# A linear-attention and gated-MLP kernel: five engines in a written order, weights decoded a whole block at a time, five PSUM banks in turn

## The chip, the cores and the metric

One core of one Trainium2 chip. The metric is the device time of one execution in microseconds (us), the median of several runs. Engine names as in the profile: PE is TensorE (matmuls; PEld its weight loads), DVE VectorE, ACT ScalarE, POOL GpSimd, SP SyncE, which here only issues transfers.

## What is computed

A recurrence per batch and head over 768 tokens, whose output feeds a gated MLP:

```python
for t in range(S):                                   # B, H, S, D = 4, 8, 768, 48
    cur = einsum('bhd,bhe->bhde', u * k[t], v[t])
    y[t] = einsum('bhd,bhde->bhe', r[t], state + cur)
    state = w * state + einsum('bhd,bhe->bhde', k[t], v[t])
x = y as (3072, 384)
out = (sigmoid(x @ w_gate) * (x @ w_val)) @ w_out    # d_ff = 1536
```

## The kernel before

**Attention.** The 768 tokens are 12 chunks of 64, and the heads 2 halves, so there are 24 *groups* `n` in order, two for a chunk. A group has these steps. `load` brings its channel-major (`chan`) and token-major (`toks`) inputs, three buffers of each. `prepare` scales queries (POOL, tile `dec`), bonus keys (four ACT instructions) and keys (DVE), and `prepare_tokens` the token-major keys (POOL). `scores` is 64 small matmuls; `keep` copies the two masked halves of the scores to SBUF (DVE); `apply` is 32 matmuls with the state (`by_state`), 32 for the state's increment (`outer`) and 32 with the scores (`by_scores`), with a drain of PE behind the first 32; `advance` updates the state (four DVE instructions); `to_x` writes the result as a high half (ACT) and a low half (DVE) into `xt`, and `fill` moves 16 rows of it with small transfers.

**MLP.** Two chunks make a *tile* of 512 columns, so there are 6 tiles. `d_ff` is 12 blocks `f`. An *item* is one block for one tile: `up` (18 matmuls of 512 columns, 9 into a gate bank and 9 into a value bank of PSUM), `gate` (sigmoid on ACT, product on DVE, high half on ACT, low half on POOL), and one item later `down` (9 matmuls into the accumulators `acc0` to `acc2`). Every product is made of three f32r matmuls of high and low halves. In tile 0 the first `HALF` = 4 blocks are done for 256 columns at a time, first for chunk 0, then for chunk 1: 8 half items, 8 whole ones.

**Weights.** They come as 64-bit words, 12 blocks of 1152 words per partition, each block in two halves of 576. For each half, `scale_words` (ACT) scales the upper 32 bits, `join_words` (three DVE instructions: a left shift with one source, then two instructions with two sources that put in sign and low bits), and `split_weights` makes the high half `whi` (ACT) and the rest `wlo` (POOL). `load_weights(f)` is issued at item f-2 and `decode(f)` follows in item f-1.

**PSUM.** `two_banks()` is a pool of two buffers, each of two banks, taken by `up`, `scores`, `apply` and small work: four banks, beside three for the accumulators.

**Order.** PE and SP run in the order in which the program is written; DVE, ACT and POOL in an order that a scheduler chose with its own estimates. SP issues every transfer: inputs, weights, `fill`, and the output. Which group goes into which item is in `SLOTS0` (tile 0) and `SLOTS` (items 0, 3, 6, 9 of the later tiles). A group's place in an item is: `up`, `scores`, `gate`, `keep`, `down` of the item before, `apply`, `to_x`, `advance`, then loads and `prepare` of the next.

Of the kernel before, what the change touches and what calls it, by code (L numbers as in the profile page):

```python
# [10 lines left out]
F32 = mybir.dt.float32  # L11
# [9 lines left out]
P = 128  # L21
# [24 lines left out]
def rwkv_then_moe(ctx: ExitStack, tc: tile.TileContext, wd, ch, tk, wt, rk0, vn0, wd0, out):  # L46
# [6 lines left out]
    op = ctx.enter_context(tc.tile_pool(name="op", bufs=2))  # L53
    ps = ctx.enter_context(tc.tile_pool(name="ps", bufs=2, space=PSUM))
# [7 lines left out]

    def two_banks():
        return ps.tile([P, 2, 512], F32, name="ring")
# [3 lines left out]
    order.enter_context(tc.manual_schedule(engines={mybir.EngineType.PE, mybir.EngineType.SP}))  # L68
# [9 lines left out]
    def load(n):  # L78
        c, g = GROUPS[n]
        chan[n] = ach.tile([P, 2, 512], F32, name="chan")  # L80
        nc.sync.dma_start(out=chan[n], in_=ch[c, g])
# [25 lines left out]
    table = const.tile([P, 1], F32, name="table")
    nc.scalar.activation(table, ident[:, 0:1], AF.Sigmoid)
# [4 lines left out]
    nc.vector.memset(pw[:, :, 0], 1.0)  # L113
    nc.vector.tensor_scalar(pw[:, :, 1], w, 0.5, 2.0, ALU.max, ALU.min)
# [18 lines left out]


    tabn = const.tile([P, N2, D], F32, name="tabn")
    flag = const.tile([1, 1], I32, name="flag")

    def token_table():
        power(32, 32, 32)
        power(64, 32, 64)  # L140
        rev = hp.tile([P, 512], F32, name="sg").rearrange("q (p a j) -> q p a j", p=NP, a=2)
        pws = pw.rearrange("q (p s) j -> q p s j", p=NP)
        nc.vector.tensor_copy(rev[0:64], pws[0:64, :, :, 95:31:-1])
        for gm in range(2):
            nc.vector.tensor_copy(rev[64:128, :, gm], pws[64:128, :, 1 - gm, 95:31:-1])
# [25 lines left out]

    W3, WH = 3 * DM, 3 * DM // 2
    raw, w32, whi, wlo = {}, {}, {}, {}

    def load_weights(f):
        for j in range(2):
            t = raw[f, j] = wp.tile([P, WH], I64, name="wr", tag=f"w{2 * f + j}")
            nc.sync.dma_start(out=t, in_=wt[f, :, j * WH : (j + 1) * WH])

    def scale_words(f, j):  # L180
        g = w32[f, j] = wtmp.tile([P, WH], F32, name="wf")
        words = raw[f, j].bitcast(F32).rearrange("q (n two) -> q n two", two=2)
        nc.scalar.activation(g, words[:, :, 1], AF.Copy, scale=2.0**-112)

    def join_words(f, j):
        words = raw.pop((f, j)).bitcast(I32).rearrange("q (n two) -> q n two", two=2)
        low, high = words[:, :, 0], words[:, :, 1]
        g = w32[f, j].bitcast(I32)
        nc.vector.tensor_scalar(g, g, 3, None, ALU.logical_shift_left)
# [3 lines left out]
    def split_weights(f):  # L193
        whi[f] = wp.tile([P, W3], F32R, name="whi", tag=f"w{2 * f}")
        wlo[f] = wp.tile([P, W3], F32R, name="wlo", tag=f"w{2 * f + 1}")
        for j in range(2):
            c, g = slice(j * WH, (j + 1) * WH), w32.pop((f, j))
            nc.scalar.copy(out=whi[f][:, c], in_=g)
            nc.gpsimd.tensor_tensor(wlo[f][:, c], g, whi[f][:, c], ALU.subtract)  # L199

    def decode(f):
        for j in range(2):
            scale_words(f, j)
        for j in range(2):
            join_words(f, j)
        split_weights(f)
# [13 lines left out]
    def prepare(n):  # L220
        c, g = GROUPS[n]
        t = dec[n] = adk.tile([P, 2, 512], F32, name="dec")
        r, k = chan[n][:, 0], chan[n][:, 1]
        tab = tabk[:, 4 * g : 4 * g + 4]
        nc.gpsimd.tensor_tensor(v4(t[:, 0]), v4(r), bc2(tab[:, :, ::-1]), ALU.mult)  # L225
# [5 lines left out]
        nc.vector.tensor_tensor(v4(k), v4(k), bc2(tab), ALU.mult)  # L231
# [29 lines left out]
    def apply(n):  # L261
        c, g = GROUPS[n]
        y = yb[n] = two_banks()
        k, v, t = toks[n][:, 0], toks[n][:, 1], score[n % 2]
        begun = set()

        def mm(half, bank, m, cs, lhsT, rhs, stop):
            first = (half, bank) not in begun
            begun.add((half, bank))
            nc.tensor.matmul(  # L270
                y[64 * half : 64 * half + m, bank, cs], lhsT, rhs,
                start=first, stop=stop, skip_group_check=True,
            )

        def by_state(half, p, p2):
            for be in range(2):
                s, row, m = half, slice(64 * be, 64 * be + D), D if half else 64
                at = (4 * (2 * g + p) + 2 * s + p2) * D
                i = (4 * p + 2 * s + p2) * C
                mm(half, be, m, slice((2 * p + p2) * C, (2 * p + p2 + 1) * C),  # L280
                       state[row, at : at + m], dec[n][row, 0, i : i + C], False)


        def outer(half, p, p2):
            for gm in range(2):
                row, at = slice(64 * gm, 64 * gm + 64), (4 * p + 2 * half + p2) * D
                m, o = D if half else 64, 256 + (2 * p + p2) * D
                mm(half, gm ^ half, m, slice(o, o + D), k[row, at : at + m],
                       v[row, at : at + D], True)

        def by_scores(half, p, p2):
            for gm in range(2):
                be, row = gm ^ half, slice(64 * gm, 64 * gm + 64)
                m, at = D if half else 64, (4 * p + 2 * be + p2) * D
                i = (4 * be + 2 * p + p2) * C
                mm(half, be, m, slice((2 * p + p2) * C, (2 * p + p2 + 1) * C),
                       v[row, at : at + m], t[row, i : i + C], True)

        units = []
        if c:  # L300
            units += [(by_state, p, p2) for p, p2 in PP]
        if c < NC - 1:
            units += [(outer, p, p2) for p, p2 in PP]
        units += [(by_scores, p, p2) for p, p2 in PP]
        turned = False
        for f, p, p2 in units:
            if f is not by_state and c and not turned:

                nc.tensor.drain()
                turned = True  # L310
            for half in range(2):
                f(half, p, p2)

    def advance(n):
        c, g = GROUPS[n]
        if c == NC - 1:
            return
        y, n2 = yb[n], 2 * D
# [380 lines left out]
```

## Time and profile before

| | |
|---|---|
| median of 3 runs | 626.62 us (626.25 to 627.57) |
| the profiled execution | 626.12 us, its span 624.1 us |
| PE busy | 543.8 us (87%), 5770 matmuls |
| PEld busy | 441.5 us (71%) |
| DVE busy | 219.9 us (35%), 365 instructions |
| ACT busy | 173.0 us (28%), 343 instructions |
| POOL busy | 201.5 us (32%), 161 instructions |
| DMA | 44.54 MB, 71 GB/s over the span |

The span runs from the first to the last instruction; the 2.0 us between it and the execution's time lie outside. A row of a timeline has start, length, engine, line, operation, tiles (written<-read) and how many were merged into it; in brackets stands the idle time before and what ended it. A row of instruction groups has the busy time in us and the mean of one in ns. PE's matmuls are pipelined, so one lasts longer than the distance to the next.

### The profile page before, as it was taken

The numbers are of one execution on the slowest core, as the hardware profiler recorded it, in microseconds if no ns is written. First come the engines' busy times: TensorE is split into PE (matmuls) and PEld (weight loads), VectorE is DVE, ScalarE is ACT, GpSimd is POOL, SyncE is SP. The second block draws the span as 40 slices with busy tenths as digits, with TensorE's granted clock in tenths as the row PEclk, the third lists the DMA queues.
The fourth block names the chain that finished last, engine by engine and source line by source line (L and its number), as shares of the span: only waits on it lengthen the run. The fifth ranks groups of instructions, "written<-read, shape, count | busy, mean of one in ns | idle before, by whom it ended". The sixth has DMA issues, their size and how long they took to land. (4 is left out here: it accounts for less than half of the span.)

```text
span 624.1 us, 13029 instructions
## 1 busy us (share of the span) xinstructions
PE 543.8 (87%) x5770; PEld 441.5 (71%) x5770; DVE 219.9 (35%) x365; ACT 173.0 (28%) x343; POOL 201.5 (32%) x161
## 2 busy tenths in 40 slices
PE   2342566879999999999999999999999999999994
PEld 2232456757787787778778778777877777888883
DVE  7832999952223313232312332222232122111011
ACT  3312445531223212132212223213233111222121
POOL 6512667751332313143213224213313111212120
PEclk9997779989999999999999999999999999999998
DMA  8025765202024002114002212010240001000001
GB/s 332 6 68 184 288 254 199 92 0 71 2 78 173 1 1 69 18 62 171 2 2 68 79 58 116 1 42 28 79 170 3 1 9 17 25 28 0 2 0 54
DMA packets 14700, 44.54 MB, mean 71 GB/s; under 512 B 2256, under 2 KB 2640, under 8 KB 14640
## 3 DMA queue, kind: packets, MB, share of 16 engines
q1 hardware_dynamic: 14640, 43.66, 20.2%
q8 instruction: 47, 0.77, 0.5%
q14 instruction: 13, 0.11, 0.0%
HBM read 36.58 MB, written 4.72 MB: 66 GB/s over the span
## 5 line engine op out<-in xcount | busy, mean ns | idle before, releaser
L386 PE MATMUL ring<-xt,whi 128*128 128x512 f32 (+1 forms) x912 | 279.2, 389 | 0.0
L386 PE MATMUL ring<-xt,wlo 128*128 128x512 f32 (+1 forms) x456 | 180.5, 396 | 34.9 <-POOL wlo L199 15.7
L386 PEld LDWEIGHTS ring<-xt,whi 128*128 128x128 f32 x912 | 173.3, 195 | 35.9 <-DVE xt L354 0.2
L399 POOL TENSOR_TENSOR h<-sg,h 128x512 fp32r<-128x512 f32 (+1 forms) x76 | 97.0, 1277 | 298.8 <-ACT h L398 298.7
L397 DVE TENSOR_TENSOR sg<-ring,sg 128x512 f32<-128x512 f32 (+1 forms) x76 | 50.3, 662 | 267.9 <-ACT sg L396 267.9
L386 PEld LDWEIGHTS ring<-xt,wlo 128*128 128x128 f32 x456 | 88.8, 195 | 54.2 <-POOL wlo L199 15.9
L409 PE MATMUL acc<-h,whi 128*128 128x512 f32 (+1 forms) x456 | 115.6, 384 | 1.2 <-POOLq L525 0.6
L396 ACT ACTIVATE sg<-ring 128x512 f32<-128x512 f32 (+1 forms) x76 | 43.7, 575 | 229.2 <-PE ring L386 229.2
L409 PEld LDWEIGHTS acc<-h,whi 128*128 128x128 f32 x456 | 84.3, 192 | 19.3 <-POOL h L399 1.3
L409 PE MATMUL acc<-h,wlo 128*128 128x512 f32 (+1 forms) x228 | 67.3, 395 | 2.5 <-ACT h L398 2.5
L398 ACT CAST h<-sg 128x512 fp32r<-128x512 f32 (+1 forms) x76 | 45.4, 598 | 54.0 <-DVE sg L397 54.0
L225 POOL TENSOR_TENSOR dec<-chan,tabk 128x512 f32<-128x512 f32 x24 | 32.7, 1364 | 80.9 <-DMA chan<-in_ch 76.6
L409 PEld LDWEIGHTS acc<-h,wlo 128*128 128x128 f32 x228 | 40.9, 190 | 12.3 <-ACT h L398 3.4
L228 ACT ACTIVATE dec<-chan,wu 128x128 f32<-128x128 f32 x96 | 31.1, 392 | 65.3 <-DMA chan<-in_ch 57.4
L199 POOL TENSOR_TENSOR wlo<-wf,whi 128x576 fp32r<-128x576 f32 x24 | 40.3, 1695 | 25.8 <-issue 11.9
L231 DVE TENSOR_TENSOR chan<-chan,tabk 128x512 f32<-128x512 f32 x24 | 19.8, 824 | 73.6 <-ACT dec L228 73.6
L255 DVE COPY_PREDICATED score<-masks,ring 128x512 f32<-128x512 int32 x48 | 35.8, 745 | 1.0 <-PE ring L247 0.3
L270 PE MATMUL ring<-score,toks 64*64 64x64 f32 (+1 forms) x768 | 18.6, 233 | 15.2 <-DVE score L255 14.4
L237 POOL TENSOR_TENSOR toks<-toks,tabn 128x384 f32<-128x384 f32 x22 | 29.2, 1332 | 6.9 <-DMA toks<-in_tk 3.8
L354 DVE TENSOR_TENSOR xt<-ring,xt 112x512 fp32r<-112x512 f32 (+1 forms) x26 | 17.9, 688 | 32.5 <-ACT xt L353 32.2
L270 PEld LDWEIGHTS ring<-score,toks 64*64 64x64 f32 (+1 forms) x768 | 15.4, 136 | 16.2 <-DVE score L255 15.4
L353 ACT CAST xt<-ring 112x512 fp32r<-112x512 f32 (+1 forms) x26 | 15.2, 586 | 39.5 <-PE ring L270 34.1
(47 smaller groups left out, 274.6 us busy)
## 6 DMA issues: line engine op xcount, KB each, us to landing
wr<-in_wt SPq DMA_DIRECT2D x24, 576.0 KB, 7.8
chan<-in_ch SPq DMA_DIRECT2D x24, 512.0 KB, 3.8
toks<-in_tk SPq DMA_DIRECT2D x24, 400.0 KB, 4.2
out_y<-o SPq DMA_DIRECT2D x18, 256.0 KB, 2.4
xt<-xt SPq DMA_DIRECT2D x30, 64.0 KB, 2.3
xt<-xt SPq DMA_DIRECT2D x12, 32.0 KB, 2.5
wu<-in_wd SPq DMA_DIRECT2D x1, 8.0 KB, 1.7
```

Source lines behind the costliest of these rows:

```text
L199: nc.gpsimd.tensor_tensor(wlo[f][:, c], g, whi[f][:, c], ALU.subtract)
L225: nc.gpsimd.tensor_tensor(v4(t[:, 0]), v4(r), bc2(tab[:, :, ::-1]), ALU.mult)
L228: nc.scalar.activation(t[:, 1, cs], k[:, cs], AF.Copy, scale=wu[:, 1, 4 * g + m : 4 * g + m + 1])
L237: nc.gpsimd.tensor_tensor(v4(k), v4(k), bc2(tabn[:, 4 * g : 4 * g + 4]), ALU.mult)
L255: nc.vector.copy_predicated(t.rearrange("q (b m i) -> q b m i", b=2, m=4), masks[:, m].bitcast(I32).unsqueeze(1).unsqueeze(1).broadcast_to ...
L270: nc.tensor.matmul(y[64 * half : 64 * half + m, bank, cs], lhsT, rhs, start=first, stop=stop, skip_group_check=True,)
L386: nc.tensor.matmul(o[:, g, self.cols], w[a][:, g * DM + kt * P : g * DM + (kt + 1) * P], self.x[:, kt, b, self.cols], start=(k == 0), stop ...
L396: nc.scalar.activation(sg[:, c], o[:, 0, c], AF.Sigmoid)
L397: nc.vector.tensor_tensor(sg[:, c], o[:, 1, c], sg[:, c], ALU.mult)
L398: nc.scalar.copy(out=h[:, 0, c], in_=sg[:, c])
L399: nc.gpsimd.tensor_tensor(h[:, 1, c], sg[:, c], h[:, 0, c], ALU.subtract)
L409: nc.tensor.matmul(self.acc[d][:, self.cols], w[a][:, 2 * DM + d * P : 2 * DM + (d + 1) * P], h[:, b, self.cols], start=(f == 0 and k == 0 ...
```

## The change

All five engines now run in a written order. For tile 0 and groups 0 to 8 it is a list of steps, `START`; for the later tiles it is a loop. The drawn-out parts of the old functions are steps of their own, with one letter each. Loads come first in the order. `fill` is issued by ACT in place of SP. The decode of blocks 1 to 11 is done on 1152 words at a time (`WHOLE`), that of block 0 in halves; the rounding and the rest stay in halves. The left shift has a second source now, a zero that is broadcast. `HALF` is 1: tile 0 has two half items and 11 whole ones. The state is decayed on ACT (four instructions) and added to on DVE (one). From group 8 on (`FIRST`) the matmuls with the state come ahead of the scores, without a drain. The ring is one PSUM tile of five banks, of which each request takes the next two, the fifth together with the first.

```diff
-HALF = 4
-SLOTS0 = {0: 2, 2: 3, 4: 4, 7: 5, 10: 6, 13: 7}
+HALF, FIRST = 1, 8
 SLOTS = (0, 3, 6, 9)
-LOADW = (-2, -1, 0, 1, 2, 3, 4, 5, 6, 7, 8, 9)
-DECW = (-1, 0, 1, 2, 3, 4, 5, 6, 7, 8, 9, 10)
+START = """
+tk tc L.0 L.1 X.0 A.0 ti.1 R.0 X.1 ti.0 A.1 R.1 k.0 W.0 tp Z.0 K.0 tt tn L.2 T.0 k.1 I.0 Z.1 h.0
+X.2 T.1 c0.0 l.0 O.0 c0.1 K.1 L.3 F.0 A.2 R.2 s.0 X.3 T.2 k.2 I.1 j0.0 Z.2 h.1 W.1 A.3 R.3 O.1
+l.1 T.3 w0.0 s.1 F.1 K.2 o0.0 W.2 k.3 I.2 j0.1 c.1 Z.3 h.2 O.2 d.2 K.3 W.3 w0.1 l.2 c.2 o0.1 s.2
+F.2 j.1 I.3 L.4 U.0 h.3 d.3 X.4 O.3 g.0 l.3 W.4 w.1 m.0 R.4 F.3 s.3 H.0 j.2 A.4 U.1 q.0 o.1 W.5
+g.1 D.0 m.1 w.2 T.4 k.4 U.2 H.1 c.3 q.1 W.6 o.2 j.3 Z.4 g.2 D.1 c.4 L.5 U.3 m.2 w.3 X.5 K.4 H.2
...
+w.9 l.6 s.6 F.6 H.7 o.9 K.7 U.8 j.10 q.7 c.11 I.7 g.8 m.8 w.10 D.7 j.11 H.8 o.10 h.7 O.7 d.7 U.9
+l.7 q.8 w.11 s.7 F.7 o.11 D.8 g.9 m.9 H.9 L.8 X.8 U.10 q.9 D.9 g.10 m.10 H.10 U.11 q.10 D.10
+g.11 m.11 H.11 U.12 q.11 A.8 R.8 k.8 T.8 D.11 g.12 m.12 H.12 q.12 D.12
+"""
...
-    wtmp = main.enter_context(tc.tile_pool(name="wtmp", bufs=3))
+    wtmp = ctx.enter_context(tc.tile_pool(name="wtmp", bufs=2))
...
+    ring = ps.tile([P, 5, 512], F32, name="ring")
+    nbank = 0
     def two_banks():
-        return ps.tile([P, 2, 512], F32, name="ring")
+        nonlocal nbank
+        b, nbank = nbank, (nbank + 2) % 5
+        return ring[:, b : b + 2] if b < 4 else ring[:, 4::-4]
...
-    order.enter_context(tc.manual_schedule(engines={mybir.EngineType.PE, mybir.EngineType.SP}))
+    order.enter_context(
+        tc.manual_schedule(engines={ET.PE, ET.SP, ET.DVE, ET.Activation, ET.Pool})
+    )
...
+    WHOLE, HALVES = (slice(0, W3),), (slice(0, WH), slice(WH, W3))
     def load_weights(f):
+        raw[f] = wp.tile([P, W3], I64, name="wr", tag=f"w{f or NF - 1}")
+        for c in HALVES if f == 0 else WHOLE:
+            nc.sync.dma_start(out=raw[f][:, c], in_=wt[f, :, c])
...
+    def join_words(f, c):
...
-        nc.vector.tensor_scalar(g, g, 3, None, ALU.logical_shift_left)
+        none = zero.broadcast_to([P, c.stop - c.start])
+        nc.vector.scalar_tensor_tensor(g, g, 3, none, ALU.logical_shift_left, ALU.bitwise_or)
         nc.vector.scalar_tensor_tensor(g, high, -(2**31), g, ALU.bitwise_and, ALU.bitwise_or)
         nc.vector.scalar_tensor_tensor(g, low, 29, g, ALU.logical_shift_right, ALU.bitwise_or)
...
     def scores(n):
         sc = ga[n] = two_banks()
+        if n >= FIRST:
+            yb[n] = two_banks()
+            from_state(n)
...
     def apply(n):
+        if n < FIRST:
+            yb[n] = two_banks()
+            if c:
+                from_state(n)
+                nc.tensor.drain()
...
+    def decay_state(n):
+        g, st = states(n)
+        for p in range(2):
+            for s in range(2):
+                nc.scalar.activation(
+                    st[:, p, s], st[:, p, s], AF.Copy,
+                    scale=pw[0:112, 4 * g + 2 * p + s, 64:65],
+                )
+    def add_state(n):
+        g, st = states(n)
+        y = yb[n][0:112, :, 256 : 256 + 4 * D].rearrange("q s (p x) -> q p s x", p=2)
+        if GROUPS[n][0]:
+            nc.vector.tensor_tensor(st, st, y, ALU.add)
+        else:
+            nc.vector.tensor_copy(st, y)
...
+    def fill(x, j, cols):
+        for lo, to in ((0, 48), (64, 112)):
+            nc.scalar.dma_start(
...
+    steps = {
+        "L": load_channels, "X": load_tokens, "W": load_weights, "A": bonus_keys, "R": queries,
+        "k": keys, "T": token_keys, "Z": scores, "K": keep, "I": apply, "O": outer,
+        "d": decay_state, "s": add_state, "h": x_high, "l": x_low, "F": fills, "D": finish,
+        "tc": constants, "tk": channel_table, "ti": inverses, "tp": token_powers,
+        "tt": token_turn, "tn": token_table,
+        "c": lambda f: [scale_words(f, c) for c in WHOLE],
+        "j": lambda f: [join_words(f, c) for c in WHOLE],
+        "w": lambda f: [round_weights(f, c) for c in HALVES],
+        "o": lambda f: [rest_of_weights(f, c) for c in HALVES],
...
+        "U": lambda i: moe_of(items[i]).up(items[i][2]),
+        "g": lambda i: moe_of(items[i]).sigmoid(items[i][2]),
+        "m": lambda i: moe_of(items[i]).product(items[i][2]),
+        "H": lambda i: moe_of(items[i]).h_high(items[i][2]),
+        "q": lambda i: moe_of(items[i]).h_low(items[i][2]),
+    }
...
+    for i in range(n0, len(items)):
...
+        m.up(f)
+        m.gate(f)
+        attend = f in SLOTS and n < 4 * (ti + 2) and n < len(GROUPS)
+        if attend:
+            scores(n)
+            if GROUPS[n][0] < NC - 1:
+                decay_state(n)
+            keep(n)
+        if i > n0:
+            finish(i - 1)
+        if attend:
+            apply(n)
+            if GROUPS[n][0] < NC - 1:
+                outer(n)
+            x_high(n)
+            x_low(n)
+            if GROUPS[n][0] < NC - 1:
+                add_state(n)
+            prepare(n + 1)
+            fills(n)
+            load(n + 2)
+            n += 1
```

The steps `c0`, `j0`, `w0` and `o0` are the halves of block 0.

More of the change, by code (lines that the diff above doesn't have):

```diff
@@ L172, in rwkv_then_moe @@
     W3, WH = 3 * DM, 3 * DM // 2
-    raw, w32, whi, wlo = {}, {}, {}, {}
+    raw, w32, wparts, whi, wlo = {}, {}, {}, {}, {}
+    WHOLE, HALVES = (slice(0, W3),), (slice(0, WH), slice(WH, W3))
     def load_weights(f):
[L176 to L183, printed above, removed]
@@ L190, in join_words @@
+    def join_words(f, c):
+        words = raw[f].bitcast(I32).rearrange("q (n two) -> q n two", two=2)
+        low, high = words[:, c, 0], words[:, c, 1]
+        g = w32[f].bitcast(I32)[:, c]
+        none = zero.broadcast_to([P, c.stop - c.start])
+        nc.vector.scalar_tensor_tensor(g, g, 3, none, ALU.logical_shift_left, ALU.bitwise_or)
         nc.vector.scalar_tensor_tensor(g, high, -(2**31), g, ALU.bitwise_and, ALU.bitwise_or)
         nc.vector.scalar_tensor_tensor(g, low, 29, g, ALU.logical_shift_right, ALU.bitwise_or)
[L193 to L206, printed above, removed]
+    def round_weights(f, c):
+        if f not in wparts:
+            wparts[f] = wp.tile([P, 2, W3], F32R, name="wx", tag=f"w{f}")
+            whi[f], wlo[f] = wparts[f][:, 0], wparts[f][:, 1]
+        nc.scalar.copy(out=whi[f][:, c], in_=w32[f][:, c])
+    def rest_of_weights(f, c):
+        nc.gpsimd.tensor_tensor(wlo[f][:, c], w32[f][:, c], whi[f][:, c], ALU.subtract)
@@ L218, in v4, with dec_of, table_of, bonus_keys @@
         return ap.rearrange("q (m t i) -> q m t i", m=4, t=2)
[L220 to L225, printed above, removed]
+    def dec_of(n):
+        if n not in dec:
+            dec[n] = adk.tile([P, 2, 512], F32, name="dec")
+        return dec[n]
+    def table_of(n):
+        return tabk[:, 4 * GROUPS[n][1] : 4 * GROUPS[n][1] + 4]
+    def bonus_keys(n):
+        t, k, g = dec_of(n), chan[n][:, 1], GROUPS[n][1]
         for m in range(4):
@@ L230, in prepare, with queries, keys, token_keys @@
             )
-        nc.vector.tensor_tensor(v4(k), v4(k), bc2(tab), ALU.mult)
-    def prepare_tokens(n):
-        c, g = GROUPS[n]
-        if c < NC - 1:
-            k = toks[n][:, 0, 0 : 8 * D]
-            nc.gpsimd.tensor_tensor(v4(k), v4(k), bc2(tabn[:, 4 * g : 4 * g + 4]), ALU.mult)
+    def queries(n):
+        t = dec_of(n)
+        nc.gpsimd.tensor_tensor(
+            v4(t[:, 0]), v4(chan[n][:, 0]), bc2(table_of(n)[:, :, ::-1]), ALU.mult
+        )
+    def keys(n):
+        k = chan[n][:, 1]
+        nc.vector.tensor_tensor(v4(k), v4(k), bc2(table_of(n)), ALU.mult)
+    def token_keys(n):
+        k, g = toks[n][:, 0, 0 : 8 * D], GROUPS[n][1]
+        nc.gpsimd.tensor_tensor(v4(k), v4(k), bc2(tabn[:, 4 * g : 4 * g + 4]), ALU.mult)
+    begun = set()
+    def into_y(n, half, bank, m, cs, lhsT, rhs, stop):
+        first = (n, half, bank) not in begun
+        begun.add((n, half, bank))
+        nc.tensor.matmul(
+            yb[n][64 * half : 64 * half + m, bank, cs], lhsT, rhs,
+            start=first, stop=stop, skip_group_check=True,
+        )
+    def from_state(n):
+        c, g = GROUPS[n]
+        for p, p2 in PP:
+            for s in range(2):
+                for be in range(2):
+                    row, m = slice(64 * be, 64 * be + D), D if s else 64
+                    at = (4 * (2 * g + p) + 2 * s + p2) * D
+                    i = (4 * p + 2 * s + p2) * C
+                    into_y(
+                        n, s, be, m, slice((2 * p + p2) * C, (2 * p + p2 + 1) * C),
+                        state[row, at : at + m], dec[n][row, 0, i : i + C], False,
+                    )
     def scores(n):
+        t, r, k = dec[n], chan[n][:, 0], chan[n][:, 1]
         sc = ga[n] = two_banks()
-        t, r, k = dec[n], chan[n][:, 0], chan[n][:, 1]
+        if n >= FIRST:
+            yb[n] = two_banks()
+            from_state(n)
         for kk, rr, at in ((k, t[:, 0], 0), (t[:, 1], r, 256)):
@@ L262, in apply @@
         c, g = GROUPS[n]
[L263 to L275, printed above, removed]
-            for be in range(2):
[L277 to L281, printed above, removed]
@@ L284, in outer @@
[L284 to L297, printed above, removed]
@@ L299, in apply @@
[L299 to L318, printed above, removed]
-        st = state[0:112, 8 * g * D : 8 * (g + 1) * D]
-        if c == 0:
-            nc.vector.tensor_copy(
-                st.rearrange("q (p a x) -> q a p x", p=2, a=2),
-                y[0:112, :, 256 : 256 + 2 * n2].rearrange("q a (p x) -> q a p x", p=2),
-            )
-            return
+        v, t = toks[n][:, 1], score[n % 2]
@@ new lines, in outer @@
+    def outer(n):
+        k, v = toks[n][:, 0], toks[n][:, 1]
+        for p, p2 in PP:
+            for be in range(2):
+                for gm in range(2):
+                    row, at = slice(64 * gm, 64 * gm + 64), (4 * p + 2 * be + p2) * D
+                    m, o = D if be else 64, 256 + (2 * p + p2) * D
+                    into_y(
+                        n, be, gm ^ be, m, slice(o, o + D), k[row, at : at + m],
+                        v[row, at : at + D], True,
+                    )
```

274 lines of the change are left out of this document (135 added, 139 removed).

## The prediction

> **What bounds the kernel now.** I read the slices of the page first, then the table of stages, then SP's timeline.
>
> ```profile
> span 624.1 us, 13029 instructions
> ...
> PE   2342566879999999999999999999999999999994
> ...
> DVE  7832999952223313232312332222232122111011
> ...
>
> ```
>
> A slice is 15.6 us. From the ninth on PE has 9 in every slice: there the kernel is PE's. In the first nine PE has 2 to 8, and from the fifth to the eighth DVE is the one with 9. Stages in numbers (time; then busy time and instructions of PE, PEld, DVE, ACT, POOL; the granted clock; DMA):
>
> ```profile
> 10.00:30.00 20.00, 8.87 (x260) 7.90 (x260) 16.79 (x22) 7.57 (x14) 11.39 (x8) 1.00 0.30 117
> 40.00:60.00 20.00, 10.46 (x205) 9.62 (x205) 5.85 (x12) 3.63 (x10) 3.50 (x4) 0.85 0.30 95
> 60.00:132.00 72.00, 46.28 (x684) 41.76 (x685) 69.59 (x91) 35.91 (x67) 48.05 (x31) 0.83 0.51 194
> 140.00:614.00 474.00, 470.70 (x4599) 376.90 (x4597) 114.74 (x217) 115.63 (x229) 123.94 (x96) 1.00 0.14 45
> ```
>
> From 40 to 60 every engine is idle more than busy; from 60 to 132 DVE has 69.6 of 72 us. SP's own queue tells why the first happens:
>
> ```profile
> 5.07 1.16 SPq L178 DMA_DIRECT2D wr<-in_wt  x2
> 27.35 4.93 SPq L358 DMA_DIRECT2D xt<-xt  x6
> 32.40 0.51 SPq L81 DMA_DIRECT2D chan<-in_ch  x1
> 49.21 4.72 SPq L358 DMA_DIRECT2D xt<-xt  x6
> 55.08 1.85 SPq L178 DMA_DIRECT2D wr<-in_wt  x4
> ```
>
> Between the second weight block (5.07) and the third (55.08) stand two `fill` batches that wait for `xt`, and everything behind them waits too. PE then sat 15.7 us for `wlo` of a block not yet loaded:
>
> ```profile
> PE ring L386 <- POOL wlo L199: 15.7, 1, 15.7
> PE ring L386 <- ACT xt L353: 10.4, 1, 10.4
> ```
>
> **What PE's work is worth when nothing is late.** One whole item without a group, then one with:
>
> ```profile
> 155.02 0.39 PE L386 MATMUL ring<-xt,wlo 128*128 128x512 f32 x1
> ...
> 161.28 0.40 PE L386 MATMUL ring<-xt,wlo 128*128 128x512 f32 x1
> ...
> 161.51 1.29 POOL L399 TENSOR_TENSOR h<-sg,h 128x512 fp32r<-128x512 f32 x1 [1.73 <-ACT h L398]
> ...
> 165.01 0.64 PE L386 MATMUL ring<-xt,whi 128*128 128x512 f32 x2
> 165.57 0.69 PE L247 MATMUL ring<-dec,chan 48*64 48x64 f32 x32
> 165.74 0.60 ACT L396 ACTIVATE sg<-ring 128x512 f32<-128x512 f32 x1 [4.31 <-PE ring L386]
> ...
> 166.37 0.69 DVE L397 TENSOR_TENSOR sg<-ring,sg 128x512 f32<-128x512 f32 x1 [5.59 <-ACT sg L396]
> ...
> 168.91 0.68 PE L270 MATMUL ring<-dec,state 48*64 48x64 f32 x32
> 169.75 0.61 PE L270 MATMUL ring<-toks 64*64 64x48 f32 x30 [0.15 <-issue]
> ...
> 170.82 0.50 PE L386 MATMUL ring<-xt,wlo 128*128 128x512 f32 x1
> ...
> 171.59 0.69 DVE L354 TENSOR_TENSOR xt<-ring,xt 112x512 fp32r<-112x512 f32 x1 [3.08 <-ACT xt L353]
> ```
>
> An item is 161.28 - 155.02 = 6.26 us, a group adds 170.82 - 161.28 - 6.26 = 3.28. The start and the end of the stretch that is PE's:
>
> ```profile
> 138.86 0.63 PE L386 MATMUL ring<-xt,wlo 128*128 128x512 f32 x1
> 615.91 0.61 PE L409 MATMUL acc<-h,whi 128*128 128x512 f32 x2
> ```
>
> At 138.86 ten items (eight of them halves) and six groups are done, so 66 items and 18 groups remain: 66 x 6.26 + 18 x 3.28 = 472.2 us. It took 616.5 - 138.9 = 477.7, a factor of 1.0116 for what is late or cold there. The whole kernel dense would be (72 x 6.26 + 24 x 3.28) x 1.0116 = 535.5; the last matmul ends at 616.5, so 81 us were lost, all before 139. That is what can be had.
>
> **The start, step by step.** I look for the time of `U.2`, the first whole item, since from there PE has work that only blocks can hold up. One row of the timeline, then groups over the whole span:
>
> ```profile
> 9.72 0.50 DVE L145 COPY sg<-pw 64x256 f32<-64x256 f32 x2
> ...
> L255 DVE COPY_PREDICATED score<-masks,ring 128x512 f32<-128x512 int32 x48 | 35.8, 745 | 1.0 <-PE ring L247 0.3
> ...
> L231 DVE TENSOR_TENSOR chan<-chan,tabk 128x512 f32<-128x512 f32 x24 | 19.8, 824 | 73.6 <-ACT dec L228 73.6
> ...
> L199 POOL TENSOR_TENSOR wlo<-wf,whi 128x576 fp32r<-128x576 f32 x24 | 40.3, 1695 | 25.8 <-issue 11.9
> ```
>
> - DVE has the tables and one key product done at 10.2; the order keeps them first.
> - Up to `s.2` it then owes four `keep` (8 x 0.745 = 6.0), three key products (2.5), four `x_low` instructions (4 x 0.69 = 2.8), three `add_state` (an estimate of 0.55 each from 0.69 for 512 columns: 1.7) and block 0 (two halves, 2.96 each by the means below: 5.9). That is 18.9 us. From 10 to 30 DVE was busy 16.79 of 20 in the same kind of chain, waiting for PE and ACT in turns, so 22.5 us: 32.7.
> - `j.1` takes 5.5 (below), `l.3` two times 0.69: 39.6. On ACT the six transfers of `F.2` stand ahead of `h.3`; SP needed 4.93 for six, and ACT has `h.3`, `d.3`, `g.0` and `w.1` behind them, some 4.5 us: about 42 for the first half of `w.1`, then two times 1.4 on POOL for `o.1` (1.29 for 512 columns at 161.51, so some 1.4 for 576).
> - So `U.2` starts at about 44. It is 40 if the chain is as tight as DVE's sum (28.9 in place of 32.7), and 50 if the issues on ACT and the copies of POOL wait for each other again. The attention loads and `W.1` have the queue free by then: `X.3` waits for `O.0`, at some 16 us, and that is the last wait ahead of `W.1`.
>
> **The decode.** In the timeline, alone and beside POOL, and as groups between 60 and 132:
>
> ```profile
> 61.22 0.46 DVE L189 TENSOR_SCALAR wf<-wf 128x576 int32<-128x576 int32 x1 [1.40 <-ACT wf L183]
> 61.71 0.76 DVE L190 SCALAR_TENSOR_TENSOR wf<-wr,wf 128x576 int32<-128x576 int32 x1
> ...
> 65.63 1.84 DVE L190 SCALAR_TENSOR_TENSOR wf<-wr,wf 128x576 int32<-128x576 int32 x1
> ...
> L190 DVE SCALAR_TENSOR_TENSOR wf<-wr,wf 128x576 int32<-128x576 int32 x20 | 21.7, 1086 | 0.4
> L191 DVE SCALAR_TENSOR_TENSOR wf<-wr,wf 128x576 int32<-128x576 int32 x20 | 20.5, 1026 | 0.3
> L189 DVE TENSOR_SCALAR wf<-wf 128x576 int32<-128x576 int32 x20 | 17.0, 849 | 1.9 <-ACT wf L183 1.8
> ...
> L397 DVE TENSOR_TENSOR sg<-ring,sg 128x256 f32<-128x256 f32 x6 | 2.5, 414 | 0.0
> ...
> 65.36 3.39 POOL L199 TENSOR_TENSOR wlo<-wf,whi 128x576 fp32r<-128x576 f32 x2 [4.69 <-DVE wf L191]
> ```
>
> The same instruction takes 0.76 while POOL is idle and 1.84 beside it. A block was 2 x (0.46 + 0.76 + 0.76) = 3.96 alone, and (21.7 + 20.5 + 17.0) / 10 = 5.92 as it came. Whole blocks: 576 more elements at some 1.07 ns (0.69 us for 512 columns on line 397, and 0.42 for 256) make 0.76 + 0.62 = 1.38, three of them 4.1. So the wider instructions save two starts and the shift with two sources gives them back: no gain alone. Beside POOL I take three chances to wait in place of six, 5.5 a block; ends 4.1 and 6.7.
>
> From 45 to the end of `j.11`: nine blocks x 5.5 = 50, ten products 6.9, four `keep` 6.0, `l` and `s` 5.0, five key products 4.1: 72, so 117, and `o.11` at 121 (at most 132 with 6.7). PE, dense from 44, wants block 11 after ten items and four groups, (62.6 + 13.1) x 1.01 = 77 us, at 121. Even; I put 6 us for waits in order (0 to 15). What hides the decode is PE's own work; were the attention of tile 0 not between the items, DVE would set the pace.
>
> **Steady part.** From 44: 71 whole items 444.5, half of a half item 1.0, 20 groups 65.6; that is 511.1.
> - The drain goes from 16 groups. It left 0.15 idle and let no matmul overlap, one small matmul's 0.2 more: 0.35 each, -5.6. Ends 0.15 and 0.5.
> - The matmuls with the state now follow `up` at once. With five banks in turn, the second bank of their result is the gate bank of that `up`. The sigmoid reads the gate bank, yet it started at 165.74, behind the 18th matmul (165.01 + 0.64) and not behind the 9th. If so after too, PE waits from 165.57 to 166.34 + 0.05: 0.8 each, 16 groups, 12.8. It is 0 if the sigmoid is let go at the 9th. I take 12.8, as the row has it.
> - Decay on ACT (four instructions) and one add in place of four on DVE, fills issued by ACT: DVE has 115 and ACT 116 of 474 us, and `up` covers 4 us of either. Nothing; up to 20 us if the 24 issues in the later tiles (4.93 / 6 = 0.82 each) hold up `gate`.
>
> Sum: 44 + (511.1 - 5.6) x 1.0116 + 6 + 12.8 = 574.2 for the last matmul; 7.6 to the end of the span as now, 2.0 outside: **584 us**. Its base is the execution of 626.1, 0.5 below the median of 626.6.
>
> **Rivals.**
> 1. *POOL and DVE shut each other out for whole instructions* (0.08). For it: the rows in which 0.76 and 1.4 us stretch each other. Against: from 60 to 132 DVE had 10 x 3.96 of decode and 2 of key products, POOL 18 x 1.4 for `wlo` and some 12 of its other work, 79 us by the lengths alone, in 72; so a tenth of it overlapped. If nothing does, 37 of `j`, 3 of keys and 48 of POOL are left at 45: `o.11` at 134, PE waits 14 in place of 6, 592. The Trainium skill (SBUF — State Buffer, "Who interferes with whom") states this very rule, for a DVE instruction with two SBUF inputs against a POOL instruction that reads SBUF; by it the zero as a second source does not free POOL from the shift, and the sum is the 592. The trace agrees with the exclusion, not quite with its length.
> 2. *The ramp stays the decode's* (0.11). For it: DVE 97% busy from 60 to 132, at 7.2 us a block. Against: PE's work beside it is now 7.6 a block. With blocks at 6.7, and half of the issues on ACT uncovered: 584 + 11 + 10 = 605.
> 3. *The sigmoid is let go at the 9th matmul* (0.26): 584 - 13 = 571. For it: it needs one bank only. Against: its row. The Trainium skill (PSUM — Partial Sum Buffer, "PSUM bank collisions raise a hardware error") asks for order by bank and 32 partitions alone; by that rule this is what would happen. The trace shows the sigmoid behind both banks.
> 4. *The ring is ordered as one tile* (0.13), the one on the other side. The sigmoid waited for both banks of its pair, so accesses may be ordered by tile, and now all five banks are one. Then the matmuls with the state wait for the product (165.57 to 167.06: 1.5), and the `up` behind a group for `x_low` and the add (170.82 to 172.28, and 0.55: 2.0). That is 3.5 x 16, and 2.0 x 4 for groups 4 to 7: 64 on 571, 635. It decides from 3.5 us a group on.
> 5. *Loads first bring nothing* (0.04): the 15.7 and 10.4 us come back as waits for DVE. Then only half items and drains are left: some 620.
>
> The forecast itself has 0.38; its bounds (40 to 50, 0 to 15, 0 to 12.8) give 561 to 597. Range 558 to 612: it holds cases 1 to 3 and leaves out 4 and 5. A difference under 0.2% can't be told from none here: same 0.02, faster 0.86, slower 0.12.
>
> **What would show it.** `U.2` near 44 and no idle time of PE over 5 us behind it; weights' transfers from 16 us on without the gap to 55; the shift at 1.4 to 2.2; in later tiles 0.8 us between `up` and the first small matmul, and no more. Wrong if PE stops some 2 us before each `up` that follows a group (rival 4), or if DVE stays at 97% until 130 with PE waiting for `wlo` (rivals 1 and 2).

## The result, and the profile after

The changed kernel takes 693.46 us (median of 4 runs, 690.47 to 695.74), the kernel before 626.43 beside it: a ratio of 1.1068, 95% interval 1.1011 to 1.1125. The forecast was 584, faster; rival 4, the one on the other side, is what came, and it came dearer than its 635. The profiled execution took 695.74 us, span 693.8.

The page of the changed kernel, slices of 17.3 us:

```profile
span 693.8 us, 12757 instructions
PE   4447886889598898988988988989879889999994
DVE  5638898941212212222122132121121221211111
PEclk9997899899798999999999989999899999999998
```

Two things differ from before. PE now has 8 and 9 by turns, with a 5 and a 7 among them, until some seven slices before the end, where before it had 9 from the tenth slice on. And DVE has 9 in two single slices only. What PE waits for (total us, times, longest):

```profile
PE ring L442 <- DVE state L381: 28.6, 14, 2.9
PE ring L287 <- DVE sg L455: 23.5, 16, 1.5
...
PE ring L442 <- DVE xt L407: 3.1, 3, 1.4
```

Line 442 is `up`, 287 the small matmuls of `apply`, 455 the product of `gate`, 381 `add_state`, 407 `x_low`. In the kernel before, the like of the first row was two waits:

```profile
PE ring L386 <- DVE state L329: 4.9, 2, 3.2
```

Its product was waited for twice too, 1.6 us in all, and these four waits all lie ahead of tile 1. Sixteen groups lie in the later tiles, and there are 16 waits of the second kind. One group in time:

```profile
257.61 4.45 PE L442 MATMUL ring<-xt,wx 128*128 128x512 f32 x18 [0.25 <-DVE total L196]
262.14 0.60 ACT L451 ACTIVATE sg<-ring 128x512 f32<-128x512 f32 x1 [4.88 <-PE ring L442]
262.77 0.69 DVE L455 TENSOR_TENSOR sg<-ring,sg 128x512 f32<-128x512 f32 x1 [5.04 <-ACT sg L451]
...
263.52 0.68 PE L287 MATMUL ring<-dec,state 48*64 48x64 f32 x32 [1.46 <-DVE sg L455]
...
267.83 0.64 PE L287 MATMUL ring<-toks 64*48 64x48 f32 x32
268.55 0.59 ACT L403 CAST xt<-ring 112x512 fp32r<-112x512 f32 x1 [3.36 <-PE ring L287]
...
269.17 0.69 DVE L407 TENSOR_TENSOR xt<-ring,xt 112x512 fp32r<-112x512 f32 x1 [2.42 <-ACT xt L403]
269.78 0.55 DVE L381 TENSOR_TENSOR state<-state,ring 112x384 f32<-112x384 f32 x1
...
270.38 6.00 PE L442 MATMUL ring<-xt,wx 128*128 128x512 f32 x18 [1.91 <-DVE state L381]
...
278.28 4.36 PE L442 MATMUL ring<-xt,wx 128*128 128x512 f32 x18
```

Read it as a chain. `up` ends at 262.06. The state's matmuls write to the fifth bank and to the gate bank of this `up`, which the sigmoid leaves at 262.74; yet they start only when DVE has read the value bank too (263.46): 1.46 us of idle PE. At 268.47 the last small matmul ends, and the next `up`, into other banks than theirs, starts only when `x_low` and `add_state` have read the small results (270.33): 1.91 more. Then the same 18 matmuls take 6.00 us in place of 4.36 to 4.45. The table of windows says why (time; busy of PE, PEld, DVE, ACT, POOL; granted clock; DMA), for that `up`, for the next one, and for everything from tile 1 on:

```profile
270.38:276.20 5.82, 5.82 (x18) 4.62 (x19) 0.65 (x1) 0.00 (x0) 0.00 (x0) 0.71 0.28 46
278.28:282.50 4.22, 4.22 (x20) 3.40 (x19) 0.00 (x0) 0.16 (x1) 1.29 (x1) 1.00 0.01 4
172.00:693.00 521.00, 453.41 (x4119) 360.30 (x4117) 100.49 (x158) 120.76 (x268) 108.79 (x88) 0.93 0.13 40
```

The same window of the kernel before:

```profile
184.00:624.00 440.00, 428.91 (x4126) 343.11 (x4124) 104.56 (x198) 105.80 (x210) 112.19 (x87) 1.00 0.14 45
```

That one comparison carries the verdict. Over the same matmuls PE is idle 521.0 - 453.4 = 67.6 us against 440.0 - 428.9 = 11.1: 56.5 more, and the three rows of waits add up to 55.2, all but 0.2 of it from tile 1 on. And its busy time is 24.5 longer at a clock of 0.93 against 1.00. Together 81 us. The slower clock is not behind every group: in the 14 that add to the state, PE stands still for 1.87 us or more ahead of the next `up`, which then mostly takes 6.00 us (5.80 to 7.13). In the last two, which add nothing, it stands for 1.44 and 1.45 us (at 569.63 and 594.01), and `up` takes 4.46 and 4.44. Tile 1's first item, in the changed kernel and in the one before:

```profile
171.91 0.40 PE L442 MATMUL ring<-xt,wx 128*128 128x512 f32 x1
```

```profile
183.43 0.40 PE L386 MATMUL ring<-xt,wlo 128*128 128x512 f32 x1
```

So the start won 11.5. From there to the end of the span it is 521.9 against 440.7, 81.2 more, and 81.2 - 11.5 is the whole difference of the spans (69.7).

The start was forecast to win far more. `U.2`, the first whole item, was put at 44 and is at 61.40:

```profile
16.09 4.32 ACTq L411 DMA_DIRECT2D xt<-xt  x6
...
40.51 9.65 ACTq L411 DMA_DIRECT2D xt<-xt  x6
...
50.25 1.17 ACT L403 CAST xt<-ring 48x512 fp32r<-48x512 f32 x2 [10.53 <-DMA xt<-xt]
...
61.40 0.94 PE L442 MATMUL ring<-xt,wx 128*128 128x512 f32 x3 [0.80 <-DVE sg L455]
```

ACT spends 9.65 us on issuing the six transfers of `F.2`, with weight loads in flight, and `h.3`, `x_high` of group 3, stands behind them for 10.53. Its first six, at 16.09, took 4.32.

### The profile page after: what moved, and what is told of

The parts are those of the page before. It is cut to its first block, busy times and chain, and to the rows that moved or that the text cites. A ratio compares the mean times of both kernels' runs of the same rounds, so it can differ in the third digit from the quotient of the medians.

```text
span 693.8 us, 12757 instructions
## 1 busy us (share of the span) xinstructions
PE 574.2 (83%) x5689; PEld 457.3 (66%) x5689; DVE 216.4 (31%) x269; ACT 189.7 (27%) x406; POOL 207.8 (30%) x159
## 5 line engine op out<-in xcount | busy, mean ns | idle before, releaser
L442 PE MATMUL ring<-xt,wx 128*128 128x512 f32 (+1 forms) x1314 | 343.4, 419 | 39.5 <-DVE state L381 28.6
L442 PEld LDWEIGHTS ring<-xt,wx 128*128 128x128 f32 x1314 | 263.3, 205 | 104.7 <-DVE state L381 30.3
L480 PE MATMUL acc<-h,wx 128*128 128x512 f32 (+1 forms) x657 | 171.7, 407 | 1.9 <-POOL h L464 1.1
L480 PEld LDWEIGHTS acc<-h,wx 128*128 128x128 f32 x657 | 125.5, 196 | 32.4 <-POOL h L464 2.0
L236 POOL TENSOR_TENSOR wx<-wf,wx 128x576 fp32r<-128x576 f32 x24 | 47.4, 1996 | 29.3 <-ACT wx L233 29.3
L287 PE MATMUL ring<-dec,state 48*48 48x64 f32 (+1 forms) x704 | 15.9, 231 | 35.7 <-DVE sg L455 23.5
L287 PE MATMUL ring<-toks 64*48 64x48 f32 (+1 forms) x704 | 17.4, 235 | 15.9 <-ACT xt L403 8.1
L318 PE MATMUL ring<-dec,chan 48*64 48x64 f32 x768 | 18.0, 239 | 12.1 <-DVE chan L274 7.5
L287 PEld LDWEIGHTS ring<-toks 64*48 64x48 f32 (+1 forms) x704 | 14.9, 148 | 18.2 <-ACT xt L403 9.3
L226 DVE SCALAR_TENSOR_TENSOR wf<-wr,wf 128x1152 int32<-128x1152 int32 (+1 forms) x13 | 25.3, 1947 | 0.4
L227 DVE SCALAR_TENSOR_TENSOR wf<-wr,wf 128x1152 int32<-128x1152 int32 (+1 forms) x13 | 24.7, 1897 | 0.5
```

The lines of the kernel that those rows point to most:

```text
L226: nc.vector.scalar_tensor_tensor(g, high, -(2**31), g, ALU.bitwise_and, ALU.bitwise_or)
L236: nc.gpsimd.tensor_tensor(wlo[f][:, c], w32[f][:, c], whi[f][:, c], ALU.subtract)
L287: nc.tensor.matmul(yb[n][64 * half : 64 * half + m, bank, cs], lhsT, rhs, start=first, stop=stop, skip_group_check=True,)
L442: nc.tensor.matmul(o[:, g, self.cols], w[a][:, g * DM + kt * P : g * DM + (kt + 1) * P], self.x[:, kt, b, self.cols], start=(k == 0), stop ...
L480: nc.tensor.matmul(self.acc[d][:, self.cols], w[a][:, 2 * DM + d * P : 2 * DM + (d + 1) * P], h[:, b, self.cols], start=(f == 0 and k == 0 ...
```

## Experiments

Two theories stood at the start for the 81 us. **A**: the program's waits are made by tile, and a ring that is one tile makes each user wait for all reads of the one before, whichever banks it uses. **B**: the banks don't matter; the new order (state matmuls ahead of the scores, `add_state` in one piece) makes the waits.

**1. One tile in the kernel before.** The written order of PE and SP is kept (the scheduler orders the others anew); only the pool of two buffers becomes one tile of four banks, taken in turn.

```diff
-    ps = ctx.enter_context(tc.tile_pool(name="ps", bufs=2, space=PSUM))
+    ps = ctx.enter_context(tc.tile_pool(name="ps", bufs=1, space=PSUM))
+    ring = ps.tile([P, 4, 512], F32, name="ring")
-        return ps.tile([P, 2, 512], F32, name="ring")
+        b, nbank = nbank, (nbank + 2) % 4
+        return ring[:, b : b + 2]
```

> The kernel before with one change: the ring is one PSUM tile of four banks, of which each request takes the next two, in place of a pool of two tiles of two banks. Theory A (accesses to one PSUM tile are ordered by tile, whatever the bank): the scores wait for the product of the same item (1.5 us) and the next up for x_low and the four state instructions (2.35 us), with 1.65 us of a lower clock behind it: 5.5 us for each of 16 to 20 groups, 715 to 735 us. Theory B (the written order of the changed kernel makes its waits, not the tile): 626 us, within 3.

Measured: 750.83 us, ratio 1.197 (1.1934 to 1.2007). The same banks in the same turns, 123 us dearer than the kernel before beside it (627.56). The waits, and one of them in time:

```profile
PE ring L391 <- DVE state L334: 70.6, 20, 9.2
```

```profile
311.73 0.66 PE L275 MATMUL ring<-score,toks 64*48 64x64 f32 x30
...
313.69 0.98 DVE L334 SCALAR_TENSOR_TENSOR state<-state,pw,ring 112x96 f32<-112x96 f32 x4
...
314.72 0.61 PE L391 MATMUL ring<-xt,wlo 128*128 128x512 f32 x1 [2.33 <-DVE state L334]
```

`up` (391) waits 2.33 us for the state's update of the group, with which it shares no bank; in the kernel before, the prediction's rows show the `up` at 170.82 starting ahead of even `x_low` at 171.59, and DVE's order around that place is the same. B is out as the main cause: B needed the new order, and it isn't there. Theory A's own figure, 715 to 735, was missed, too: it had the scores wait for the product. In the trace it is the sigmoid that waits for the scores (it starts at 307.51, behind them), so the product, `keep` and the matmuls behind `keep` come later, and PE's waits for the copied scores are 33.1 us where the kernel before has 14.4.

**2. Five tiles of one bank in the changed kernel.** Instructions that took both banks become two: `keep`, `add_state`, `x_high` and `x_low`.

```diff
-    ring = ps.tile([P, 5, 512], F32, name="ring")
+    ring = [ps.tile([P, 512], F32, name=f"ring{b}") for b in range(5)]
-        return ring[:, b : b + 2] if b < 4 else ring[:, 4::-4]
+        return ring[b], ring[(b + 1) % 5]
```

> The changed kernel with one change: the five banks are five PSUM tiles of one bank each; instructions that read two banks become two. Theory A: the waits for product and add vanish. From tile 1 on it takes what before took from there, 433 us less 6 for the drains, and tile 0 at most its 172 us, some 10 less if the same waits go there: 590 to 612 us. Theory B: the waits stay, over 680 us. And if order by tile is also why the sigmoid started behind the 18th matmul, it now starts behind the 9th.

Measured: 600.02 us, 0.9578 (0.9549 to 0.9606): 93 us less for splitting one tile into five, although that takes more instructions. The first matmul of tile 1, and one group:

```profile
160.41 0.40 PE L445 MATMUL ring<-xt,wx 128*128 128x512 f32 x1
...
270.41 4.36 PE L445 MATMUL ring<-xt,wx 128*128 128x512 f32 x18
272.76 0.60 ACT L454 ACTIVATE sg<-ring 128x512 f32<-128x512 f32 x1 [2.83 <-PE ring L445]
274.70 0.68 PE L287 MATMUL ring<-dec,state 48*64 48x64 f32 x32
274.88 0.69 DVE L458 TENSOR_TENSOR sg<-ring,sg 128x512 f32<-128x512 f32 x1 [5.59 <-PE ring L445]
...
278.99 0.64 PE L287 MATMUL ring<-toks 64*48 64x48 f32 x32
279.56 4.44 PE L445 MATMUL ring<-xt,wx 128*128 128x512 f32 x18
```

And its window from tile 1 on:

```profile
161.00:596.00 435.00, 423.17 (x4117) 340.35 (x4115) 100.81 (x219) 120.95 (x284) 108.68 (x88) 0.99 0.15 48
```

The sigmoid starts 2.35 us into `up`, behind the ninth matmul; no wait is left between `up`, the small matmuls and the next `up`, which takes 4.44; the clock is 0.99. From tile 1's start to the end of the span it takes 596.0 - 160.4 = 435.6 us in place of 521.9.

**3. The state's matmuls late, with the drain, in all groups.** The kernel of experiment 2 (kernel 2 from here) with `FIRST` at 24; from group 8 on they read a state that ACT has decayed already, so it computes other numbers.

```diff
-HALF, FIRST = 1, 8
+HALF, FIRST = 1, 24
...
-    n = FIRST
+    n = 8
```

> As a_banks, but the matmuls with the state stand in apply in all groups, with a drain behind them. Theory A with my price of the drain: 16 x 0.35 = 6 us slower than a_banks. If the early place costs a wait for the sigmoid (0.8 us x 16 = 13), it is 7 us faster.

Measured: 607.48, 0.9672 (0.9642 to 0.9702), 7.5 over kernel 2. Forecast for the drains was 16 x 0.35 = 5.6. In the trace the drain shows behind the state's matmuls:

```profile
284.58 0.68 PE L287 MATMUL ring<-score,toks 64*64 64x64 f32 x32 [0.24 <-issue]
```

So putting these matmuls first gains, once tiles are apart.

**4. `fill` issued by SP again,** in kernel 2 and, one tile left as it is, in the changed kernel.

```diff
     def fill(x, j, cols):
-            nc.scalar.dma_start(
+            nc.sync.dma_start(
```

> As a_banks, but fill is issued by SP again, at the same place of the written order. In the changed kernel x_high of group 3 waited 10.5 us on ACT behind six such transfers, and U.2 started at 61 in place of 44. If it is ACT's queue that cost this: 5 to 12 us faster than a_banks. If the transfers land late whoever issues them, since three weight blocks are in flight: within 3 us of a_banks.

> The changed kernel with one change: fill is issued by SP. With one tile for the ring the early waits stay, so if the two causes add: 693 less the 13 us between a_banks and a_banks_sp, 680. If the ring's waits hide the fills: 690 or more.

Measured: 586.62, 0.936 (0.9336 to 0.9384), 13.4 under kernel 2; and 683.64, 1.0908 (1.0873 to 1.0943), 9.8 under the changed kernel. The sign is the same with either ring. The first gain is a little more than the 5 to 12 that were expected; the second lies between 680, the additive time, and the 690 of the other view. In the first of them the six issues, and `U.2`:

```profile
30.96 3.84 SPq L414 DMA_DIRECT2D xt<-xt  x6
...
44.91 1.42 PE L445 MATMUL ring<-xt,wx 128*128 128x512 f32 x5 [1.85 <-POOL wx L236]
```

The same two in kernel 2:

```profile
35.91 11.29 ACTq L414 DMA_DIRECT2D xt<-xt  x6
...
56.72 0.96 PE L445 MATMUL ring<-xt,wx 128*128 128x512 f32 x3 [0.22 <-POOL wx L236]
```

So 11.8 us lie ahead of `U.2`, of 12.2 between the spans of the two profiled executions.

ACT as such isn't the slow one. Its first six took 4.32 us in the changed kernel and 4.21 in kernel 2, while the DMA engines were busy for 0.52 and 0.61 of that time; the six of `F.2` took 9.65 and 11.29, with the DMA engines busy throughout (a share of 1.02 in both). SP's six at 30.96 met a share of 0.17, because on SP the weight loads stand behind them and go out at 35.94. What differs is thus the moment; whether SP would take as long beside running loads, no run shows.

**5. `fill` issued by ACT in the kernel before,** the same edit the other way round.

> The kernel before with one change: fill is issued by ACT, so that SP's loads no longer stand behind it. My reading of before: the third weight block waits from 5 to 55 us for this alone, and PE loses 15.7 us to it: 600 to 612 us. Rival: the decode has the pace, so blocks that come earlier only wait for DVE: over 620.

Measured: 611.77, 0.9767 (0.9736 to 0.9798): 14.5 faster. SP's queue and the stage from 60 to 132:

```profile
5.13 1.18 SPq L178 DMA_DIRECT2D wr<-in_wt  x2
...
31.16 3.85 SPq L178 DMA_DIRECT2D wr<-in_wt  x4
```

```profile
60.00:132.00 72.00, 54.51 (x770) 47.09 (x770) 61.04 (x82) 33.46 (x65) 47.29 (x33) 0.88 0.41 146
```

The third weight block is issued at 31.16 in place of 55.08, and PE has 54.5 of those 72 us in place of 46.3. One edit, two signs. In the kernel before, `fill` waits on SP for `xt`, blocks loads that are needed, and moving it to ACT pays. In the new order the loads behind it on SP go out at 35.94 (24.56 with `fill` on ACT), and from 30 us on ACT waits for none of them; on ACT, `fill` meets running loads and holds up `x_high` and the decode.

**6. The decode, four ways.** All have five tiles and `fill` on SP. The first puts the shift with one source back, the second goes back to halves for scaling and joining, the third does both (the decode of before in the new order), the fourth has the first and also rounds and takes the rest on whole blocks.

```diff
-        nc.vector.scalar_tensor_tensor(g, g, 3, none, ALU.logical_shift_left, ALU.bitwise_or)
+        nc.vector.tensor_scalar(g, g, 3, None, ALU.logical_shift_left)
...
-        "j": lambda f: [join_words(f, c) for c in WHOLE],
+        "j": lambda f: [join_words(f, c) for c in HALVES],
...
-        "w": lambda f: [round_weights(f, c) for c in HALVES],
-        "o": lambda f: [rest_of_weights(f, c) for c in HALVES],
+        "w": lambda f: [round_weights(f, c) for c in WHOLE],
+        "o": lambda f: [rest_of_weights(f, c) for c in WHOLE],
```

> As a_banks_sp, but the left shift has one source again (whole blocks stay). Between 45 and 110 us DVE is busy 60 and POOL 57 of 65 us, and PE has some 15 us of waits for them. If a shift with two sources costs what its length says (1.63 us by its mean against 0.9 for two halves' worth before alone) and the ramp pays it: 0.6 to 1 us for each of 9 blocks, 5 to 9 us faster, 578 to 582. If DVE and POOL only trade waits: within 2 us of a_banks_sp's 586.6.

> As a_banks_sp, but scale and join in halves in all blocks (the shift keeps two sources). My prediction: wider instructions save two starts a block, 0.14 us each alone, and three chances to wait beside POOL: halves 2 to 5 us slower. The other view: a shorter instruction is interrupted less and lets whi and wlo of the first half start 3 us earlier: 2 to 5 us faster.

> As a_banks_sp with both undone: halves, and the shift with one source. If the two add up, the sum of the two differences before it. It is the decode of the kernel before in the new order.

> As sp_shift, but round and rest also on whole blocks (blocks 1 to 11): one start less on ACT and POOL and one chance less to wait for DVE in each block, as whole blocks brought for scale and join: 2 to 5 us faster than its 582.6. If the later start of the rest counts more (POOL begins 0.7 us later): the same or slower.

| | whole words | halves |
|---|---|---|
| shift with two sources | 586.62 | 596.63 (0.952; 0.9497 to 0.9543) |
| shift with one source | **582.58** (0.9281; 0.9244 to 0.9317) | 592.33 (0.945; 0.941 to 0.9491) |

Rounding and rest on whole blocks too: 586.83 (0.9363; 0.9338 to 0.9387), 4.2 over the 582.58. Whole words gain 10.0 and 9.8, the second source costs 4.0 and 4.3: they add up, within the intervals. Of the expectations, the shift's 5 to 9 and the halves' 2 to 5 missed in size, and that whole blocks for rounding and rest would gain 2 to 5 missed in sign. The groups between 45 and 110, first with two sources and whole words, then with one:

```profile
L236 POOL TENSOR_TENSOR wx<-wf,wx 128x576 fp32r<-128x576 f32 x15 | 33.2, 2232 | 4.1 <-ACT wx L233 4.1
L227 DVE SCALAR_TENSOR_TENSOR wf<-wr,wf 128x1152 int32<-128x1152 int32 x8 | 18.2, 2271 | 0.3
L226 DVE SCALAR_TENSOR_TENSOR wf<-wr,wf 128x1152 int32<-128x1152 int32 x7 | 16.7, 2389 | 0.2
L225 DVE SCALAR_TENSOR_TENSOR wf<-wf,zero 128x1152 int32<-128x1152 int32 x7 | 12.1, 1724 | 4.0 <-ACT wf L218 4.0
```

```profile
L236 POOL TENSOR_TENSOR wx<-wf,wx 128x576 fp32r<-128x576 f32 x17 | 30.1, 1792 | 8.9 <-ACT wx L233 8.9
...
L225 DVE TENSOR_SCALAR wf<-wf 128x1152 int32<-128x1152 int32 x8 | 10.9, 1365 | 4.0 <-ACT wf L218 4.0
```

The shift itself gets 0.36 us shorter, and POOL's rest (236), which isn't touched, 0.44 a half: the second source cost both engines. With POOL idle the shift takes 1.35 us with two sources (at 31.37 in the first kernel) and 0.75 with one (at 31.12 in the second), so the one-source shift, at 1.37 on average, is stretched beside POOL as well. The Trainium skill (SBUF — State Buffer, "Who interferes with whom") has DVE and POOL share a pair of ports under an exclusive lock; the direction agrees, with the differences above as its measure here. In halves a block takes DVE more, not less:

```profile
L225 DVE SCALAR_TENSOR_TENSOR wf<-wf,zero 128x576 int32<-128x576 int32 x13 | 18.4, 1412 | 1.4 <-ACT wf L218 1.4
L226 DVE SCALAR_TENSOR_TENSOR wf<-wr,wf 128x576 int32<-128x576 int32 x13 | 17.6, 1354 | 0.4
L227 DVE SCALAR_TENSOR_TENSOR wf<-wr,wf 128x576 int32<-128x576 int32 x13 | 15.0, 1151 | 0.5
```

2 x (1.41 + 1.35 + 1.15) = 7.8 us a block against 1.72 + 2.39 + 2.27 = 6.4. The last kernel's rest takes 2.98 for a whole block, less than 2 x 1.79:

```profile
L236 POOL TENSOR_TENSOR wx<-wf,wx 128x1152 fp32r<-128x1152 f32 x8 | 23.9, 2983 | 12.4 <-ACT wx L233 12.4
```

It is still slower. Two things in its trace can be the reason: a rest that starts only when the whole block is rounded (POOL's idle time behind ACT's rounding grows from 8.9 to 12.4), and a DVE that takes longer beside the longer rest (the one-source shift 1.90 in place of 1.37, the three instructions of a block 6.3 in place of 5.8). No run takes these apart.

The kernel with five tiles, `fill` on SP, whole words and the one-source shift, 582.58 us, beats both kernels.

## Why the prediction was wrong

In three stretches, the forecast's own terms against the runs (us; "tiles" is experiment 2, "tiles + SP" the first of 4). The forecast's later tiles are (60 x 6.26 + 16 x 3.28 - 5.6) x 1.0116 + 12.8 + 7.6; what is left between is tile 0.

| | forecast | changed | tiles | tiles + SP |
|---|---|---|---|---|
| `U.2` starts | 44 | 61.4 | 56.7 | 44.9 |
| from there to tile 1 | 90 | 110.5 | 103.7 | 103.7 |
| from there to the end of the span | 447.8 | 521.9 | 435.6 | 435.2 |
| span | 581.8 | 693.8 | 596.0 | 583.8 |

- **The step that failed: PE's wait in the later tiles, put at 0.8 x 16 = 12.8 us, up to the moment when the sigmoid has left the gate bank.** That is a wait by bank: the state's matmuls share the gate bank with `up`, so the sigmoid alone holds them. What came instead is a wait for every reader of the one tile, the product, `x_low` and the add: 56.5 us more of idle PE, and 24.5 of slower matmuls behind it. The prediction had the row that tells it, at 165.74: the sigmoid starts behind the 18th matmul though it needs the first nine. So the reader waited for matmuls into a bank that it doesn't read, and that bank and its own were of one tile. With all five banks in one tile, that is rival 4. The row was quoted there, and the chance stayed at 0.13, while rival 3, with the account by banks that the Trainium skill gives (PSUM — Partial Sum Buffer, "PSUM bank collisions raise a hardware error"), got twice as much though its only row spoke against it. Experiments 1 and 2 decide it from both sides: +123 us with the one tile in the old order, -93 without it in the new. The sign that was named for rival 4, PE stopping some 2 us before each `up` behind a group, is the 1.91 of the trace.
- **Rival 4's size.** Its 3.5 us a group is what PE's idle time shows (56.5 / 16 = 3.5: 1.5 for the product, 2.0 for `x_low` and the add). What it lacked is the clock: PE's busy time is 24.5 longer, 1.5 a group on average and some 1.6 in each of the 14 groups with an `up` of about 6.0 us. Its 2.0 x 4 for the groups of tile 0 stands beside 110.5 - 103.7 = 6.8.
- **Rival 3 was right about the program and wrong about this kernel.** The sigmoid is let go at the ninth matmul when its bank is a tile of its own; then the wait is 0, not 0.8, and the later tiles take 435, which is the forecast without its 12.8. Here the steady arithmetic (6.26 an item, 3.28 a group, the factor 1.0116) holds to a microsecond.
- **Decay on ACT and fills issued by ACT, put at nothing, up to 20.** For the fills, as a sum over the run, the upper bound held 9.8 and 13.4. The place was wrong: not 24 issues in the later tiles, but six in the start. They were priced at SP's 4.93, from a moment when the DMA engines were busy for 0.14 of the time, and cost ACT 9.65 beside weight loads; what stood behind them was the chain to `U.2`.
- **`U.2` at 44** is right as a chain of DVE, ACT and POOL: 44.9 as soon as ring and fills are put right. In the changed kernel it is 17.4 late: 4.7 by the one tile, 11.8 by the fills (56.7 to 44.9 in the table), 0.9 by the chain. That the chain came out so near is in part luck, as the forecast had the fills on ACT in it, at 4.93 us.
- **The decode at 5.5 a block and `o.11` at 121 with 6 us of waits** was too short: in the first kernel of experiment 4 a block takes 6.4, `o.11` ends at 128.6, and the stretch from `U.2` to tile 1 takes 13.7 more than forecast. Of these, by the table of windows, PE's busy time is 6 longer than the dense 84 of the forecast (90.1, at a clock of 0.97), and its idle time is 13.6 in place of 6. Only 2.2 of the idle time is a wait for weights; most of the rest is for other results of POOL and DVE (3.8 for `h`, 2.3 for `score`, 2.2 for the product). Between 45 and 110 both engines are nearly full there:

```profile
45.00:110.00 65.00, 53.79 (x707) 40.78 (x708) 60.22 (x54) 33.63 (x66) 57.50 (x28) 0.95 0.38 151
```

  DVE has 60.2 and POOL 57.5 of 65 us, so rival 2 (the start stays the decode's) was right about that stretch, at 6.4 rather than 6.7; its other half, 10 us for issues on ACT, stands beside the 11.8. "No gain alone", said of wide words with the two-source shift while POOL is idle, holds: three times 1.35 to 1.36 is 4.1, against the 3.96 of two halves. Beside POOL a gain was forecast (5.5 in place of 5.92) and came: halves with one source are 592.33, whole words with two 586.62. Only the level was off, for both. Whether a third buffer for `wf` would help, no run shows (between 45 and 110 ACT's scaling waits 12.3 us for POOL's rest).
- **The drain, 5.6:** from tile 1 to the end of the span went from 624.1 - 183.4 = 440.7 to 435.6, 5.1 less; and putting it back, with the old place of the matmuls, cost 7.5. Both lie within its bounds (0.15 to 0.5 a group, 2.4 to 8.0 in all); neither run changes the drain alone.
- **Rival 5** is out: experiment 5 gets 14.5 us from clearing SP's queue alone, and the start won 11.5 even in the changed kernel.
- **A slip of reading:** PE has 9 from the tenth slice on (140 us), not from the ninth; no sum hangs on it.

The 586.62 of the kernel with both faults undone lies near the forecast of 584 by chance: 13.7 missing in tile 0 against 12.8 too many for the sigmoid.

## What to carry to other kernels

Give each PSUM bank that is handed out by itself a tile of its own; a reader that starts behind a bank it doesn't read is the sign that the order goes by tile. Price a stall of PE with what it does to the clock behind it, here 1.5 us a group on top of 3.5. Before moving a transfer's issue to another queue, list what stands behind it on both queues at that place: the same move gained 14.5 us in one order and cost 13.4 in the other.

## What the runs showed of the hardware

- Behind two stalls of 1.46 and 1.91 us, 5 us apart, with small matmuls and the nine of `down` between them, the granted clock is 0.71 for the next 5.8 us. Behind stalls of 1.47 and 1.44 us, and of 1.47 and 1.45, in the last two groups, the next `up` takes 4.46 and 4.44; those groups have 32 small matmuls fewer between the stalls. The Trainium skill (TensorE: Matmul & The Clock Gate, "What's actually happening") lets the clock fall to half after an idle window of about 3.4 us. No stall here is that long, so the trace doesn't agree with the condition. It agrees with the size: by an estimate from that page, one window of 3.4 us at half clock would cost 1.7 us, and the `up` lost 6.00 - 4.45 = 1.55. What the clock gate counts is left open.
- Six small issues cost ACT 9.65 and 11.29 us while weight loads kept the DMA engines busy throughout, and 4.32 and 4.21 while these were busy for 0.52 and 0.61 of the time; SP took 3.84 at a share of 0.17.
- With POOL idle, DVE's shift with two sources takes 0.75 us on 576 words (at 26.24 in the first kernel of experiment 4) and 1.35 on 1152; between 45 and 110, beside POOL, it takes 1.41 and 1.72 on average. So the share of waiting in a short instruction is the larger one there.
